# A two-layer attention and token-mixing kernel: the written-out order of its operations is replaced by another

## The chip, the cores and the metric

The kernel runs on one core of a Trainium2 chip. The metric is device time in microseconds of one execution, from the median of several runs. A core has five engines that work at the same time, each through its own list of instructions in order: TensorE (PE in the profile; its weight loads are PEld), VectorE (DVE), ScalarE (ACT), GpSimd (POOL) and SyncE (SP), which here only issues transfers. Engines wait for one another by semaphores.

## The reference

One sequence of 2048 positions and 512 features passes twice through the same two blocks. All tensors are bfloat16.

```python
x = x + A(layernorm(x), wqkv, wo)          # 32 heads of 16, window of 256
x = x + B(layernorm(x), w1, b1, w2, b2)    # mixes along the sequence
...
# A: causal attention in a sliding window
mask = (i - j >= 0) & (i - j < 256)
p = softmax(where(mask, q @ k.T * Dh**-0.5, -1e9))
o = p @ v ; return o @ wo
# B: MLP over positions, 1792 hidden
h = layernorm(x)
u = gelu(einsum("bsd,sf->bdf", h, w1) + b1)
y = (einsum("bdf,fs->bds", u, w2) + b2).transpose(0, 2, 1)
```

## The kernel before

All of x stays on the chip as 16 tiles of 128 positions. Each layer runs as follows.

*Normalising.* For each tile VectorE takes the statistics (L478, L480), GpSimd raises the variance to the power -1/2 (L491), VectorE scales (L498). Transposed tiles, xhT, come from DMA transposes (L549), and for the first two tiles from TensorE (L556) with a copy on ScalarE (L569) or VectorE (L567).

*Projections.* TensorE multiplies (L520, the helper through which nearly all full-size matmuls go). Results leave PSUM by a cast of queries (VectorE L585, ScalarE L587), of keys (L610, L612) and of values (L651, L653). Keys are spread into a block-diagonal form, kbd, either straight from PSUM (VectorE L600, ScalarE L595) or from a staging tile by GpSimd or VectorE (L626) or by eight small transfers (L620). Values pass through transfers too (L656).

*Attention.* The queries are cut into chunks of 256 or 512 positions. For each chunk and each group of heads TensorE makes scores into two pairs of PSUM banks (L710, four matmuls side by side in the rows of the array, each with two heads' keys of 64 positions), ScalarE takes the exponential of each pair (L725), GpSimd or VectorE masks the blocks at the window's edges (L746), TensorE multiplies by the values (L767), and VectorE transposes and divides (L787, L791, L793, L798; L793 can be GpSimd's). The output projection is L520 again, added to x by VectorE (L809).

*Mixing.* The product with w1 is cut along the sequence. Parts of it are computed while attention still runs and are kept in float32 in space that is free then (L520, taken out by L873, L875 or L877), so that TensorE has something to do when it would wait for ScalarE; the last part is L888, added by VectorE (L899) and passed through gelu by ScalarE (L903). The product with w2 is L520 again and is added to x by VectorE (L929, and L915 for the last tile, which is cut into three). In the second layer the tiles of the first layer's w2 product feed the next attention chunk by chunk. Weights w1 and w2 are loaded by SP (L823, L835) into a few buffers; results leave by L976 and L918.

*The order.* A recorder, `Graph`, collects 2475 operations with what they read, write and which buffer pool they take from. Many have `alts`, the same work on another engine. It makes no schedule: `begin_order` unpacks a list that is stored in the text of the kernel, and `replay` walks it. Each entry says which operation comes next and which of its alternatives is taken:

```python
for lo, hi in zip(raw[:n], raw[n:]):
    k, alt = divmod(lo + 256 * hi, 4)
    out.append((left.pop(k), alt))
...
o.eng, o.fn = o.alts[alt][:2]
self._take(o)
```

The walk decides three things: the order in which each engine's instructions stand, the engine of each operation with alternatives, and, since `_take` hands out a pool's free buffers as they come, which buffer each tile gets and so what it must wait for. `emit` then writes each engine's list with the semaphore waits that follow. SP's list is in this order too.

Of the kernel before, what the change touches and what calls it, by code (L numbers as in the profile page):

```python
# [11 lines left out]
P = 128  # L12
# [3 lines left out]
    'c-pmAO^D;>8GhyYy!%bif~F{-fC>sIpnw*%paliApn?`eaX={wXu$^^RPezI4!Gce11h-S4Jx?cg99!o;D8S<%)tj2TyVevALihL3qH7D${c)fVGa}UVGe!e'  # L16
    '@yvK;XR`}QUR$>O>HB-1_j#VrH7;(%00h2#X_%&=>n}cksz0Tk2Vk1EX&Hv`iD8(utAhsG<N7upJFc@>=H|qqw)+_=`-P%!jz**0r@4`-nWh4wsI@wYAPQtK'
    '90-EYmyXXR8q7(V3tu!yv(@By{kYvTIvwBjip8j49@$)h<K#fD<eZOkN48@agxD?-MQ|J<%bdW$`q2f;VXzn+I|b<XJN@GeNebxM*%_s+)oN8JG-95=0MFw$'
    'E=)`U<I(I;o==DK6FQttDV@z`<JF1=fjpj!JOAkP!Iua*O9VQh<S)xbEdmivP6T0GBn6Cqzc0&4ASWb;+a*nNVzMlWX)Dggh{mgGy=GN}rXWaAt5F)&W`s;8'
    '6GFWLaa@<nXM!-Wd=C*7z5jMQIoIuh(Q!T3Xby*F(s!Kaz8~AZZ(0a^QFk20ex7r4x|4HsJ?HAr*e5K@Yr3YW0E#Tj<Rk<NT~$pwodnu=4}vI(_{npC<;3_s'  # L20
    'VSV4HETxXKU|9<@QdO0zhgm5rD{>8YD2TNh$FpoYpjw6IIc%fMtm>uGf1<^55k)1h4Xbq}jv+1&=ZnSn!{M;eXn6CJ$;6%v&GA^*`-72g^$@0h7>;}4aM<nk'
    'x)$zXFc=hz`mr8%Ue)Wm-e@!%UpFFMujO*NW(|K<Dkfs7eW6yW_+mB3`6FA6s_V6?us&Y~e!eM{T#Q1o5J321yFa^!*d$nOoP}lSlc&NTmP<nb`6I%OF|FT<'
    's-ZsC06Eg(njFgm{HBHxRilX5HpMz%_<jJg=X<`HqNOVNPZTFd2&X8>c~jm{q|~|05*?o|#BOKMLEKxN6P07%mnEr5NmQ@Lag?pI;6+fOEcih{yp8XiuWKvc'
    '_dHcm@$x)M;0S=@Ii3Ooy`C;yfUYM=a(0G9R(P4msVDs(ewYvcby)#?#`bz`fDY*-xPfnKe`}DK)GdVGB43#1pQ_cDm6v1B^Fq(JEDwxNZQEuswd%7<jQ|gl'
    'loEmG`5p(wioqG&V9Ih^ZiJ$PiL%^rrKiNGeQ<I?>;|@7335I-R;URC65%8<97oI9YT)RGs_QnVSeh|YrWM;>@U}cv<Ow$(BN${3Euq<LN--{IMOGA970L<H'
    'siOs0&MH{tie*^>T7#l1{HYwmux+WQl#a*oNH7OsSgm&B*ckQu)#{*DsYqxVqL79tk{VdSS6?Y{smgMXbp2@<hFng=0$;G3&7%Mzd@-FO*|C^;KM(U$A_0e~'
    'GW{eu%xbEps-!@OuIq?|>lTquPjWd_7AnnxC&88vmI)wo9HS_dq9i0pyRSA!r}}(0pU=@6^(-h^SylU^5eiQxSpwp>60m%o<BG-N=xZpo+kcm&&1M4)D9feN'
# [982 lines left out]
```

## Time and profile before

| | |
|---|---|
| median of the runs | 435.45 us |
| profiled execution | 435.28 us, of which 433.5 us is the span of its instructions |
| TensorE busy | 421.4 us, 6177 matmuls |
| VectorE busy | 315.7 us, 611 instructions |
| ScalarE busy | 319.0 us, 366 instructions |
| GpSimd busy | 186.3 us, 282 instructions |
| granted TensorE clock | 1.00 |
| transferred by SP's queue | 45.52 MB |

Busy is the time in which at least one instruction of the engine was under way. Matmuls overlap in their pipeline, so a gap between two of them that is shorter than the tail of the first does not show as idle time. An idle engine costs nothing unless it is the one on which the end depends; which one that is changes along the kernel, so the stages are read one by one.

### The profile page before, as it was taken

What the parts mean: (1) busy time and instruction counts of PE and PEld (TensorE: products, weight loads), DVE (VectorE), ACT (ScalarE), POOL (GpSimd) and SP (SyncE); (2) the same over time, 40 slices, a digit from 0 to 9 for tenths busy, and PEclk for the clock granted to TensorE, in tenths of its full rate; (3) what the DMA queues carried; (4) which work ended last, traced back from release to release, by engine and by line L of the source; (5) the groups of instructions that cost most, each with busy time, mean ns of one, the idle gap of its engine ahead of it and who ended that gap; (6) DMA issues with size and microseconds to landing.
All of it is one profiled execution on the core that took longest, in us unless ns stands there. A gap on an engine that the chain in (4) does not pass through costs nothing.

```text
span 433.5 us, 14319 instructions
## 1 busy us (share of the span) xinstructions
PE 421.4 (97%) x6177; PEld 188.8 (44%) x6177; DVE 315.7 (73%) x611; ACT 319.0 (74%) x366; POOL 186.3 (43%) x282
## 2 busy tenths in 40 slices
PE   8889989999999999999999999999999999999997
PEld 7444333434444444444444444444434444444544
DVE  7999888878995988544878898699779667522223
ACT  6999999999997853606999999899999970601000
POOL 4987877455554310010444656776565331000000
PEclk9999999999999999999999999999999999999999
DMA  8983413401064166735472432251222346856514
GB/s 249 175 151 75 87 33 80 101 14 39 15 178 120 52 177 170 215 75 146 107 128 64 95 81 42 50 89 22 45 65 76 88 122 183 218 150 178 149 49 132
DMA packets 104091, 46.44 MB, mean 107 GB/s; under 512 B 34396, under 2 KB 104028, under 8 KB 104028
## 3 DMA queue, kind: packets, MB, share of 16 engines
q1 hardware_dynamic: 104028, 45.52, 42.8%
q8 instruction: 49, 0.80, 0.8%
q14 instruction: 14, 0.11, 0.1%
HBM read 33.56 MB, written 2.10 MB: 82 GB/s over the span
## 4 chain that ended last, share of the span: by engine, by line
PE 83%; ACT 15%; DVE 1%; POOL 1%; issue 0%; POOLq 0%
PE PS L520 57%; ACT pt L725 15%; PE PS L710 9%; PE PS L888 8%; PE PS L767 8%; DVE rl L787 0%; DVE stats L478 0%; DVE xh_sb L498 0%; POOL rstd L491 0%; PE PS L556 0%; PE PS L392 0%; DVE agg L480 0%; POOL ldm L442 0%; DVE ldm L443 0%; DVE x_sb L915 0%
## 5 line engine op out<-in xcount | busy, mean ns | idle before, releaser
L725 ACT ACTIVATE pt<-PS 128x1024 bf16<-128x1024 f32 (+1 forms) x304 | 280.8, 1043 | 10.9 <-PE PS L710 9.8
L746 POOL TENSOR_TENSOR pt<-pt,ldm 128x256 int32<-128x256 int32 (+2 forms) x195 | 128.9, 683 | 90.0 <-ACT pt L725 89.6
L520 PE MATMUL PS<-uT,w2b 128*128 128x512 bf16 (+2 forms) x308 | 69.7, 360 | 0.0
L520 PE MATMUL PS<-xhT,wqkv 128*128 128x512 bf16 (+1 forms) x288 | 67.3, 357 | 2.1 <-ACT pt L725 2.0
L520 PE MATMUL PS<-xh_sb,w1b 128*128 128x512 bf16 x280 | 69.0, 381 | 0.1
L710 PE MATMUL PS<-qT,kbd 32*128 32x64 bf16 (+4 forms) x1552 | 60.2, 247 | 3.5 <-ACT pt L725 1.5
L491 POOL TENSOR_TENSOR rstd<-agg,mhalf 128x2 f32<-128x2 f32 (+1 forms) x33 | 23.1, 703 | 74.8 <-DVE agg L480 74.7
L929 DVE SCALAR_TENSOR_TENSOR x_sb<-PS,bcol,x_sb 128x512 bf16<-128x512 f32 x31 | 22.7, 743 | 39.6 <-PE PS L520 39.6
L787 DVE STREAM_TRANSPOSE rl<-PS 128x1024 f32<-128x1024 f32 x32 | 39.9, 1246 | 14.8 <-PE PS L767 14.7
L710 PEld LDWEIGHTS PS<-qT,kbd 32*128 32x128 bf16 x1552 | 22.5, 92 | 62.4 <-ACT pt L725 47.5
L903 ACT ACTIVATE uT<-rl,bcol 128x512 bf16<-128x512 f32 x28 | 18.4, 713 | 40.7 <-DVE rl L899 40.7
L767 PE MATMUL PS<-pt,vb 64*17 64x128 bf16 (+4 forms) x3104 | 43.8, 248 | 2.3 <-ACT pt L725 0.8
L478 DVE BATCH_NORM_STATS2 stats<-x_sb 128x6 f32<-128x512 bf16 x64 | 42.9, 683 | 0.7
L520 PEld LDWEIGHTS PS<-uT,w2b 128*128 128x128 bf16 x308 | 27.8, 98 | 32.0 <-issue 3.2
L520 PE MATMUL PS<-uT,pt 128*128 128x512 bf16 x168 | 40.9, 379 | 0.0
L767 PEld LDWEIGHTS PS<-pt,vb 64*17 64x17 bf16 x3104 | 31.6, 84 | 17.6 <-issue 7.0
L888 PE MATMUL PS<-xh_sb,w1b 128*128 128x512 bf16 x168 | 38.1, 379 | 0.0
L520 PEld LDWEIGHTS PS<-xh_sb,w1b 128*128 128x128 bf16 x280 | 23.8, 98 | 31.2 <-issue 5.9
L520 PEld LDWEIGHTS PS<-xhT,wqkv 128*128 128x128 bf16 x288 | 23.6, 97 | 29.1 <-issue 6.7
L520 PE MATMUL PS<-wqkv,xhT 128*128 128x512 bf16 x128 | 34.0, 381 | 0.0
L520 PE MATMUL PS<-wo_sb,oT 128*128 128x512 bf16 x128 | 32.7, 381 | 0.6 <-ACT pt L725 0.5
L498 DVE TENSOR_SCALAR xh_sb<-x_sb,agg,rstd 128x512 bf16<-128x512 bf16 x64 | 25.7, 421 | 5.5 <-POOL rstd L491 5.4
(63 smaller groups left out, 336.5 us busy)
## 6 DMA issues: line engine op xcount, KB each, us to landing
w1b<-in_B_w_dram SPq DMA_DIRECT2D x112, 128.0 KB, 2.8
w2b<-in_B_w_dram SPq DMA_DIRECT2D x70, 128.0 KB, 2.7
pt<-in_B_w_dram SPq DMA_DIRECT2D x42, 128.0 KB, 2.9
vb<-vst SPq DMA_DIRECT2D x64, 68.0 KB, 2.1
out_dram<-x_sb SPq DMA_DIRECT2D x15, 128.0 KB, 1.8
x_sb<-in_A_x_dram SPq DMA_DIRECT2D x3, 512.0 KB, 5.8
kbd<-stg SPq DMA_DIRECT2D x88, 16.0 KB, 1.9
wqkv<-in_A_wqkv_dram SPq DMA_DIRECT2D x4, 256.0 KB, 4.8
```

What stands on the lines that cost most here:

```text
L478: op("vector:stat", lambda e: e.bn_stats(st[:, 0:6], x_sb[:, t, :]), reads=[f"x{t}"], writes=[("st", i)], cost=dve_cost(512))
L491: op("gpsimd:rstd", lambda e: e.tensor_tensor(rstd[:, t0:t1, 0], agg[:, t0:t1, 1], mhalf[:, 0:1].to_broadcast([P, t1 - t0]), op=ALU.pow), ...
L498: op("vector:xh", lambda e: e.tensor_scalar(xh_sb[:, t, :], x_sb[:, t, :], agg[:, t, 0:1], rstd[:, t, :], op0=ALU.subtract, op1=ALU.mult), ...
L520: return e.matmul(o, lhsT=w, rhs=x, start=start, stop=stop, skip_group_check=True)
L710: last = e.matmul(bank(tt[r // 2], r % 2)[:, base + c0 * 64:base + (c0 + n) * 64], lhsT=kbd[32 * r:32 * r + 32, tk.slot, o, jj].rearrange( ...
L725: op("scalar:exp", lambda e, ts=ts, tp=tp, i=i, cols=cols: e.activation(probs(tp)[:, i, 0:cols, :], pair(ts)[:, :, 0:cols].rearrange("p r ...
L746: return e.tensor_tensor(v, v, m, op=by)
L767: last = e.matmul(bank(t, h)[32 * r:32 * r + 17, i + q0 * 64:i + (q0 + n) * 64], lhsT=vb[64 * h:64 * h + 64, tk.slot, jj, 4 * o + r, :], r ...
L787: op("vector:od", lambda e, t=tod, tr=tr: e.transpose(rl[:, tr.slot:tr.slot + 2].rearrange("p a b -> p (a b)"), pair(t)), reads=[(tod, i) ...
L888: last = e.matmul(bank(tu, tt), lhsT=v()[:, sc - b0, k0 + tt * P:k0 + (tt + 1) * P], rhs=xh_sb[:, sc, :], start=(sc == b0), stop=(sc == NT ...
L903: op("scalar:gelu", lambda e, ft=ft, tt=tt: e.activation(uT[:, ft, :], rl[:, tmps[tt].slot], ACTF.Gelu_apprx_tanh, bias=b1col[:, ft:ft + 1 ...
L929: op("vector:resy", lambda e: e.scalar_tensor_tensor(x_sb[:, t, :], bank(ft), b2col[:, t:t + 1], x_sb[:, t, :], op0=ALU.add, op1=ALU.add), ...
```

## The change

Nothing but the packed list `ORDER` is replaced: another sequence of the same 2475 operations, with other alternatives chosen for some of them.

```diff
 ORDER = (
-    'c-pmAO^D;>8GhyYy!%bif~F{-fC>sIpnw*%paliApn?`eaX={wXu$^^RPezI4!Gce11h-S4Jx?cg99!o;D8S<%)tj2TyVevALihL3qH7D${c)fVGa}UVGe!e'
...
+    'c-pmAPl)U05g*y#CSQscw4etHXo~`RMFqd2fKn7tK?@2f;D8GXIG}(Idf<Q$4!EEc6<lz^1qT%H!3P(7a6tz@@WBNid~m@B7hLec0Uum&VGr-%!XA8B${srM'
...
 )
```

Unpacked, it comes to this:

| engine | instructions before | after |
|---|---|---|
| TensorE | 6177 | 6177 |
| VectorE | 611 | 630 |
| ScalarE | 366 | 361 |
| GpSimd (without the constants of the preamble) | 278 | 266 |
| SP (transfers) | 438 | 422 |

Of the masks (L746), 60 move from GpSimd to VectorE and 43 from VectorE to GpSimd. Of the products (L793), four go to VectorE and seven to GpSimd. Casts of queries move both ways, four and four; three casts of values and two key expansions move from ScalarE to VectorE; one transposed tile's copy moves from VectorE to ScalarE. Weight loads (L823, L835) and outputs (L976, L918) are issued in another order.

50 lines of the change are left out of this document (25 added, 25 removed).

## The prediction

> **What bounds the kernel now.** I read the page first: busy time and the chain that ended last.
>
> ```profile
> span 433.5 us, 14319 instructions
> ...
> PE 421.4 (97%) x6177; PEld 188.8 (44%) x6177; DVE 315.7 (73%) x611; ACT 319.0 (74%) x366; POOL 186.3 (43%) x282
> ...
> PE 83%; ACT 15%; DVE 1%; POOL 1%; issue 0%; POOLq 0%
> ```
>
> TensorE is occupied for nearly the whole span and carries 83% of the chain; ScalarE has 15%. The profiled execution took 435.28 us, 1.78 more than its span, and the median of the runs shown is 435.45. All sums below start from 435.28. Next I asked for busy time in the stages of the kernel. The columns are length of the stage, then busy time (and instructions) of each engine.
>
> ```profile
> 0.00:9.40 9.40, 8.23 (x82) 7.13 (x83) 6.27 (x25) 5.92 (x9) 4.03 (x15) 1.00 0.78 230
> 9.40:24.00 14.60, 12.57 (x199) 7.06 (x197) 14.03 (x36) 14.60 (x22) 11.99 (x21) 1.00 0.97 218
> 24.00:71.00 47.00, 42.04 (x990) 18.26 (x990) 41.73 (x80) 46.57 (x52) 36.52 (x52) 1.00 0.41 80
> 71.00:126.00 55.00, 54.04 (x1052) 22.38 (x1052) 48.36 (x91) 54.29 (x60) 32.38 (x48) 1.00 0.24 54
> 126.00:157.00 31.00, 31.00 (x587) 13.75 (x581) 25.05 (x49) 27.01 (x29) 11.30 (x15) 1.00 0.41 115
> 157.00:201.00 44.00, 44.00 (x295) 20.18 (x285) 26.63 (x49) 13.26 (x20) 2.26 (x4) 1.00 0.60 162
> 201.00:308.00 107.00, 106.97 (x1791) 44.41 (x1792) 89.01 (x174) 102.40 (x117) 62.19 (x92) 1.00 0.37 75
> 308.00:318.00 10.00, 9.37 (x182) 3.98 (x175) 6.56 (x12) 9.83 (x12) 5.25 (x7) 1.00 0.23 44
> 318.00:354.00 36.00, 35.98 (x656) 15.23 (x653) 26.84 (x52) 34.81 (x38) 18.97 (x28) 1.00 0.34 88
> 354.00:389.00 35.00, 35.00 (x171) 15.88 (x163) 18.45 (x33) 8.32 (x13) 1.38 (x2) 1.00 0.64 177
> 389.00:433.50 44.50, 42.17 (x224) 20.49 (x221) 12.77 (x19) 1.95 (x3) 0.00 (x0) 1.00 0.44 131
> ```
>
> Two regimes stand here. From 9.4 to 126 us ScalarE is full: 14.60 of 14.60, 46.57 of 47, 54.29 of 55 us. After 126 us TensorE is full, except for 0.63 us in 308 to 318 (10.00 - 9.37). The granted clock is 1.00 in every row. The chain in order of time (start, length, what) says the same:
>
> ```profile
> 24.76 9.28 ACT pt L725 x10
> ...
> 43.39 27.65 ACT pt L725 x30
> ...
> 99.16 9.28 ACT pt L725 x10
> ...
> 308.31 9.28 ACT pt L725 x10
> ...
> 389.23 41.95 PE PS L520 x222
> ```
>
> Exponentials (L725) set the time early, at 0.93 us each, with one late patch at 308 us; the rest is matmuls, and the last 42 us is nothing else.
>
> From the stages comes the most that better order can give. TensorE's idle time between its start and its tail is 14.60 - 12.57 = 2.03, 47.00 - 42.04 = 4.96, 55.00 - 54.04 = 0.96, then 0.03, 0.63 and 0.02: 8.63 us in all, 2.0% of 435.28. And most of it can't be had, because it lies where ScalarE is full. ScalarE's own idle time there is 0 + 0.43 + 0.71 = 1.14 us.
>
> **What the change does.** Only the packed list ORDER differs, so I listed both programs engine by engine. TensorE has the same 926 steps, the same 6177 matmuls and the same 337 changes between the three shapes of matmul (projections and MLP, scores L710, probabilities times values L767). The 152 score steps stand in the same sequence. Before 157 us 304 of 311 TensorE steps stand within five places of where they stood. So this is no new plan, it is the old one with neighbours exchanged, and the work of the bounding engine is unchanged: 0 us.
>
> What moves: 60 masks (L746) go from GpSimd to VectorE and 43 the other way; 11 products (L793) change engine; some PSUM evacuations change between VectorE and ScalarE (ScalarE issues 361 instructions instead of 366); two groups of eight key transfers (L620) leave SP's queue, 438 to 422 transfers; and the weight loads (L823, L835) are issued in another order.
>
> **Start-up.** The first exponential starts at 9.40. What leads to it:
>
> ```profile
> 5.71 0.59 ACT L569 COPY xhT<-PS 128x512 bf16<-128x512 bf16 x1 [0.60 <-PE PS L556]
> 5.93 0.61 PE L556 MATMUL PS<-ident,xh_sb 128*128 128x128 bf16 x4
> 6.58 0.42 DVE L567 COPY xhT<-PS 128x512 bf16<-128x512 bf16 x1
> 7.10 1.91 PE L520 MATMUL PS<-xhT,wqkv 128*128 128x256 bf16 x16
> 7.74 0.84 ACT L595 ACTIVATE kbd<-PS,par 128x256 bf16<-128x256 f32 x2 [1.44 <-PE PS L520]
> 8.46 0.37 ACT L587 CAST qT<-PS 128x256 bf16<-128x256 f32 x1
> 8.94 0.40 PE L710 MATMUL PS<-qT,kbd 32*128 32x256 bf16 x12
> 9.40 1.02 ACT L725 ACTIVATE pt<-PS 128x1024 bf16<-128x1024 f32 x1 [0.56 <-PE PS L710]
> ...
> 12.44 0.42 ACT L587 CAST qT<-PS 128x256 bf16<-128x256 f32 x1
> 12.69 4.33 ACT L725 ACTIVATE pt<-PS 128x1024 bf16<-128x1024 f32 x5
> ...
> L600 DVE TENSOR_TENSOR kbd<-PS,par 128x512 bf16<-128x512 f32 x3 | 2.0, 669 | 0.0
> ```
>
> After the change the second copy of xhT is made by ScalarE, 0.59 instead of 0.42, so the first projection starts 0.17 later, at 7.27. In exchange VectorE expands the keys (one L600 of 0.67) while ScalarE casts the query. The second projection step ends 0.6 us of pipeline and 0.44 us of issue after 7.27, at 8.31; the cast of 0.37 ends at 8.72, and L710 starts at 8.82 where it started at 8.94: -0.12. One later cast of a query (12.44 to 12.69, 0.25 us from start to start) leaves ScalarE altogether; since ScalarE is full, that is worth -0.25. One step that could give this back: two score steps now follow each other near 16 us where two projections stood between, but TensorE waits for ScalarE there anyway. Together -0.37; the bounds are 0 and -0.6 (nothing, or both parts and one more such cast).
>
> **The patch at 308 us.** The last exponentials of a chunk hold up L767 for the 0.63 us of TensorE idle time above. The new order puts two w1 steps, four matmuls, ahead of that group, which is more than fills the gap. Three evacuations of values and one of keys also leave ScalarE in 157 to 308:
>
> ```profile
> L653 ACT CAST vst<-PS 128x512 bf16<-128x512 f32 x8 | 4.9, 610 | 15.6 <-PE PS L520 15.6
> L595 ACT ACTIVATE kbd<-PS,par 128x512 bf16<-128x512 f32 x2 | 1.3, 685 | 1.6 <-PE PS L520 1.6
> ```
>
> At 610 and 685 ns these are 3 x 0.61 + 2 x 0.69 = 3.2 us of ScalarE, but TensorE is full where they leave, so they buy slack and no time; if that cover were gone they would be worth their 3.2 us. Between 0 and -0.63 I take -0.4.
>
> **Masks and the two queues.** A mask moved is a mask queued behind other work.
>
> ```profile
> L746 POOL TENSOR_TENSOR pt<-pt,ldm x195: 449/727/1523, 12.6 to 351.4; 128x256 int32<-128x256 int32 x139, 128x128 int32<-128x128 int32 x47, 128x384 int32<-128x384 int32 x9
> L746 DVE TENSOR_TENSOR pt<-pt,ldn x71: 228/414/690, 36.0 to 352.8; 128x256 int32<-128x256 int32 x51, 128x128 int32<-128x128 int32 x17, 128x384 int32<-128x384 int32 x3
> ...
>   PEld PS L767: 2.0, 4
>   PE PS L767: 0.6, 1
> ```
>
> (Duration is least/median/most in ns; below, who waited for masks.) VectorE takes 17 more in net: 2 in the first layer, 15 in the second. At 0.414 us that is 7.0 us more for VectorE and 17 x 0.727 = 12.4 us less for GpSimd. The densest place is 24 to 71 us, where nine masks come to VectorE and two leave: 41.73 + 7 x 0.414 = 44.6 of 47 us. It fits, though what is queued behind a mask there (evacuations of q, k and v, without which a bank isn't free) comes up to 0.69 us later. In the second layer 89.01 + 10 x 0.414 + 4 x 0.69 = 95.9 of 107. Waits for masks cost at most 2.0 us in the whole kernel; I bound the change by that, from -2.0 to +2.0. Since ScalarE doesn't wait for masks but for scores, a short lateness is caught by TensorE's idle time. I take +0.2.
>
> A rule of the Trainium skill speaks against these moves. "SBUF — State Buffer", in its section "SBUF: two separate sides", says that VectorE and GpSimd share one pair of ports, and that a VectorE instruction with two SBUF inputs and a GpSimd instruction that reads SBUF exclude one another for a whole instruction. The trace bears it out only in the tail: the longest VectorE mask, 690 ns, is 276 over the median of 414, and the median is not stretched.
>
> **Transfers.** The new order issues w1 and w2 nearer to their use. What the trace has of them (w1; time to landing least/median/most):
>
> ```profile
> L823 SPq DMA_DIRECT2D w1b<-in_B_w_dram x112: 340/469/1832, 15.4 to 375.2; - x112
> ...
>   PEld PS L520: 0.5, 1
> ...
> DMA to landing us min/median/max: 2.0/2.8/4.6
> ```
>
> One wait of 0.5 us in 112 loads; a load can land 4.6 - 2.8 = 1.8 us later than usual. SP works in order, so a load behind a transfer that still waits for its data waits too: the key transfers, the transposes (L549), and at the end the outputs (L976) behind L929. Late loads would stop TensorE in 157 to 201 or after 354, where nothing covers it. Below, nothing is gained (-0.5, the one wait); above, one load at its latest, +1.8. I take +0.2, as one in 112 was late. The two groups of key transfers that leave SP free its queue early; that is cover for the transposes and no time.
>
> **The end.** The last TensorE group is now seven matmuls of 128 columns instead of five. Ahead of the last small output stands another whole tile's output (L976) where a half tile's (L918) stood.
>
> ```profile
> 431.17 0.81 SPq L918 DMA_DIRECT2D out_dram<-x_sb  x2
> ```
>
> SP needs 0.81 / 2 = 0.4 us to issue one. Between 0 (the last result is later than that) and +0.4 (it waits for a whole issue) I take +0.1; a gain is excluded, since the last group is no shorter.
>
> **Sum:** 435.28 - 0.37 - 0.4 + 0.2 + 0.2 + 0.1 = 435.0 (-0.1%). With all lower ends: 435.28 - 0.6 - 0.63 - 2.0 - 0.5 = 431.6. With all upper ends: 435.28 + 2.0 + 1.8 + 0.4 = 439.5.
>
> **Rivals.**
>
> *The waits only change places.* Each one removed comes back for a neighbour: 435.3. For it: the score sequence is identical and ScalarE stays full from 9.4 to 126. It can't be told from the forecast by time alone.
>
> *VectorE and GpSimd exclude each other.* If each of the 17 extra masks is held for the 276 ns that the longest shows, and TensorE sees all of it, it is 17 x 0.276 = 4.7 us, so 435.0 + 4.7 = 439.7. It decides as soon as VectorE in 24 to 71 us passes 47 us: 44.6 + 9 x 0.276 = 47.1, just there. Against it: only few masks were stretched before. This is the rule of "SBUF — State Buffer" in the Trainium skill, taken at its worst.
>
> *Weight loads come late (the other side).* SP's queue, in 157 to 201 and after 354: if loads are issued so close that a landing of 4.6 instead of 2.8 us stops TensorE each time, five such stops are 5 x 1.8 = 9.0 and one more 0.5: 435.0 + 9.5 = 444.5. It decides when the margin between landing and first use falls under 1.8 us. Against it: a single wait before, and transfers at 0.60 and 0.64 of the DMA engines there.
>
> *TensorE's idle time closes.* All 8.63 us, and the start-up's 0.37: 426.3. For it: the search had the whole order to choose from. Against it: ScalarE is full where 7.95 of the 8.63 us lie, and its work there falls by one cast.
>
> **How the numbers follow.** Forecast 0.60, waits change places 0.16, exclusion 0.15, late loads 0.06, idle time closed 0.03. The range that leaves out no more than 2 in 10 joins the first three: 432.0 to 439.7. Two per cent of 435.45, about what a measurement of this kernel can tell from no change, is 8.7 us. Faster than 426.7 is only the last case, 0.03; slower than 444.2 only late loads, 0.06; within that the rest, 0.91.
>
> **What would show it.** In the new profile: TensorE's count stays 6177 and its busy time is within 2 us of 421.4; the first L725 starts near 9.3; ScalarE stays over 98% busy from 24 to 126 us; TensorE's idle time in the patch near 308 us falls under 0.3; VectorE's total rises to about 324 us and GpSimd's falls to about 178; waits of TensorE for masks stay under 4 us, for weight loads under 2. I am wrong if the ScalarE-bound stretch ends more than 2 us away from 126, or if TensorE shows gaps in 157 to 201 or after 354.

## The result, and the profile after

The changed kernel takes 437.10 us (median of six; 436.80 to 437.38). The kernel before, on the same chip, takes 435.45 us as the median of five runs; a sixth run of it took 591.89 us and is left out. The ratio is 1.0037, 95% interval 1.0023 to 1.0051: slower by about 1.6 us, where 0.3 us less was forecast. The profiled execution took 437.18 us, 1.90 more than that of before. First the page after:

```profile
span 435.4 us, 14241 instructions
...
PE 412.6 (95%) x6109; PEld 188.1 (43%) x6177; DVE 326.7 (75%) x630; ACT 317.4 (73%) x361; POOL 182.4 (42%) x270
...
PE 72%; ACT 18%; DVE 3%; DMA 2%; issue 2%; POOL 1%; SPq 1%
```

All 6177 weight loads are there, but the records of 68 matmuls are not, so TensorE's busy time is not compared with the 421.4 of before; starts of weight loads are used instead. What can be read: VectorE, a transfer, GpSimd and "issue" now stand in the chain with 8% together, where they had 2%. The same stages as in the prediction (length, then busy time and instructions of each engine) show where:

```profile
9.40:24.00 14.60, 12.71 (x221) 7.41 (x221) 14.29 (x36) 14.48 (x21) 11.36 (x20) 1.00 1.01 213
24.00:71.00 47.00, 40.17 (x937) 17.69 (x940) 42.21 (x84) 45.63 (x50) 31.59 (x45) 1.00 0.47 84
71.00:126.00 55.00, 52.15 (x1018) 22.10 (x1018) 46.88 (x82) 54.37 (x60) 38.74 (x58) 1.00 0.26 54
...
308.00:318.00 10.00, 9.75 (x218) 4.31 (x201) 7.96 (x14) 9.84 (x12) 3.59 (x6) 1.00 0.24 46
```

ScalarE, the bound there, lost 0.94 us in 24 to 71 (46.57 to 45.63) and nothing in 71 to 126 (54.29, 54.37). Its timeline (start, length, what; in brackets the idle time before) names the moments. Before:

```profile
24.76 18.44 ACT L725 ACTIVATE pt<-PS 128x1024 bf16<-128x1024 f32 x20 [0.24 <-PE PS L710]
43.39 3.77 ACT L725 ACTIVATE pt<-PS 128x1024 bf16<-128x1024 f32 x4 [0.19 <-PE PS L710]
```

After:

```profile
23.31 4.68 ACT L725 ACTIVATE pt<-PS 128x1024 bf16<-128x1024 f32 x5
28.30 5.60 ACT L725 ACTIVATE pt<-PS 128x1024 bf16<-128x1024 f32 x6 [0.31 <-PE PS L710]
34.20 3.77 ACT L725 ACTIVATE pt<-PS 128x1024 bf16<-128x1024 f32 x4 [0.29 <-PE PS L710]
38.46 5.61 ACT L725 ACTIVATE pt<-PS 128x1024 bf16<-128x1024 f32 x6 [0.49 <-PE PS L710]
44.34 2.86 ACT L725 ACTIVATE pt<-PS 128x1024 bf16<-128x1024 f32 x3 [0.28 <-PE PS L710]
```

One run of 20 exponentials has become runs of 6, 4 and 6: three holes, each a wait for scores. Exponentials in a run start 0.905 us apart; by starts the holes are 0.47, 0.45 and 0.63 us. (I call hole what a distance has over 0.905.) Both kernels have a fourth, at 43.4 and 44.3. All holes over 0.1 us from 24 to 126 us sum to 2.4 us before and 3.9 after, without the place near 118 us where a copy stands between two exponentials.

The sequence of score steps is the same in both kernels, so their starts make a ledger. Stretches are cut at score steps that start at 8.9, 19.7, 26.0, ... us in the kernel before; each entry is the longer (+) or shorter (-) time of the stretch against the kernel before, worked out from the starts in the traces. The rows with numbers are the experiments below:

| profile | 0–8.9 | –19.7 | –26.0 | –46.4 | –66.5 | –121.7 | –205.8 | –313.1 | –349.7 | –last weight load | sum |
|---|---|---|---|---|---|---|---|---|---|---|---|
| after | -0.15 | -0.34 | -0.01 | **+1.52** | +0.12 | +0.10 | -0.20 | +0.01 | +0.30 | +0.42 | +1.76 |
| after, 2nd profile (15) | -0.39 | -0.35 | -0.01 | **+1.45** | +0.12 | +0.17 | -0.22 | +0.44 | +0.29 | +0.39 | +1.90 |
| 1 start new, rest old | +0.10 | -0.35 | -0.01 | +2.41 | 0.00 | -0.06 | +0.36 | 0.00 | +0.04 | +0.01 | +2.49 |
| 2 middle old | +0.58 | -0.30 | -0.01 | +1.73 | +0.12 | +0.08 | -0.20 | -0.01 | +0.30 | +0.18 | +2.47 |
| 3 copy first | +0.83 | -0.34 | -0.01 | **+0.83** | +0.13 | +0.16 | -0.22 | -0.03 | +0.29 | +0.30 | +1.94 |
| 4 w2 piece early | +0.08 | -0.16 | -0.01 | +1.36 | +0.12 | +0.10 | -0.23 | +0.15 | +0.29 | +0.21 | +1.89 |
| 5 large load later | -0.39 | -0.35 | -0.01 | **+0.78** | +0.12 | +0.22 | -0.15 | +0.52 | +0.29 | +0.04 | +1.09 |
| 6 before, copy late | +0.04 | 0.00 | 0.00 | **+0.86** | +0.01 | +1.65 | +0.13 | -0.04 | +0.03 | +0.01 | +2.70 |
| 7 before, large load late | 0.00 | 0.00 | +0.02 | +0.04 | +0.01 | +0.05 | -0.04 | -0.02 | +0.03 | 0.00 | +0.08 |
| 8 four repairs | -0.30 | -0.14 | +0.14 | +0.61 | +0.12 | +0.08 | +0.27 | +0.41 | +0.29 | 0.00 | +1.48 |
| 9 six repairs | +0.21 | -0.34 | -0.01 | +0.84 | +0.12 | +0.14 | +0.33 | +0.02 | +0.29 | +0.32 | +1.93 |
| 10 seven repairs | +0.57 | -0.35 | -0.01 | +1.67 | +0.10 | +0.07 | -0.22 | -0.02 | +0.30 | +0.11 | +2.23 |
| 11 less on VectorE | -0.23 | +0.13 | -0.01 | +1.32 | +0.10 | +0.14 | -0.09 | 0.00 | +0.30 | +0.25 | +1.90 |
| 12 no hurry last | -0.32 | +0.75 | -0.01 | **+0.01** | **+2.51** | +0.10 | -0.15 | +0.04 | +0.29 | +0.23 | +3.44 |
| 13 loads as before | -0.36 | +0.05 | -0.01 | +1.50 | +0.12 | +0.16 | -0.22 | +0.01 | +0.29 | +0.46 | +1.99 |
| 14 before, new loads | +0.50 | +0.46 | -0.03 | +0.05 | 0.00 | 0.00 | +1.11 | -0.01 | +0.03 | +0.01 | +2.12 |
| 16 run 9, then before | +0.82 | -0.35 | -0.01 | +0.84 | +0.12 | +7.79 | -0.08 | -0.02 | +0.01 | 0.00 | +9.11 |

Rows are single executions. Where the order up to a place is the same, 26 to 46 us gives +1.36 to +1.52 (after, 15, 4, 13), and the stretches that end at 66.5, 121.7 and 349.7 agree within 0.2 us. The others do not repeat: the first two lie between -0.39 and +0.83 and between -0.35 and +0.75 in thirteen profiles of one and the same start, and 122 to 313 us and the tail differ by up to 0.6 us. Of the 1.76 us of the changed kernel 1.52 are made in 26 to 46 us; 0.30 lie in 313 to 350, 0.42 in the tail.

What is late at each hole? Hole 1, TensorE:

```profile
26.41 0.46 PE L767 MATMUL PS<-pt,vb 64*17 64x64 bf16 x27
27.28 0.64 PE L767 MATMUL PS<-pt,vb 64*17 64x256 bf16 x37 [0.41 <-issue]
```

It stops after 27 of the 64 products that stand there in a row, ahead of its 345th weight load of the program, and waits for nothing that the profile shows. Weight loads there are 0.76 us apart, and the score step stands right behind. Hole 2: a score step behind a product of L767 that waited for a GpSimd mask. Hole 3: a score step behind projections that waited for a copy of queries on VectorE. The table of waits from 24 to 46 us has the last two (total, times, longest), and the two timelines show why the copy, L585, was late: two normalizations stand ahead of it.

```profile
PE PS L520 <- DVE qT L585: 0.8, 1, 0.8
...
PE PS L767 <- POOL pt L746: 0.6, 1, 0.6
```

```profile
33.83 1.25 DVE L787 STREAM_TRANSPOSE rl<-PS 128x1024 f32<-128x1024 f32 x1 [0.64 <-PE PS L767]
35.01 1.37 DVE L498 TENSOR_SCALAR xh_sb<-x_sb,agg,rstd 128x512 bf16<-128x512 bf16 x2
36.30 0.68 DVE L585 CAST qT<-PS 128x512 bf16<-128x512 f32 x1
```

```profile
37.04 1.04 PE L520 MATMUL PS<-xhT,wqkv 128*128 128x512 bf16 x4 [0.83 <-DVE qT L585]
38.01 0.40 PE L710 MATMUL PS<-qT,kbd 32*128 32x192 bf16 x12
```

The two normalizations are also longer than usual. VectorE in the kernel before, then GpSimd in the changed one:

```profile
34.49 0.74 DVE L498 TENSOR_SCALAR xh_sb<-x_sb,agg,rstd 128x512 bf16<-128x512 bf16 x2
```

```profile
35.05 1.19 POOL L746 TENSOR_TENSOR pt<-pt,ldm 128x128 int32<-128x128 int32 x2
```

The same pair takes 0.74 us there and 1.37 here, where two GpSimd masks run beside it. One by one they last 0.64 and 0.81 us, and each ends 0.15 us after one of the masks ends (masks 35.50 and 36.23, normalizations 35.65 and 36.38). So 0.63 us of the copy's lateness is VectorE held up beside GpSimd. That is read from the durations; no run below moves these two masks away.

Counted by how late the score steps are, the 1.52 us are about 0.4 around hole 1, 0.35 around hole 2 and 0.8 around hole 3.

### The profile page after: what moved, and what is told of

The parts are those of the page before. It is cut to its first block, busy times and chain, and to the rows that moved or that the text cites. A ratio compares the mean times of both kernels' runs of the same rounds, so it can differ in the third digit from the quotient of the medians.

```text
span 435.4 us, 14241 instructions
## 1 busy us (share of the span) xinstructions
PE 412.6 (95%) x6109; PEld 188.1 (43%) x6177; DVE 326.7 (75%) x630; ACT 317.4 (73%) x361; POOL 182.4 (42%) x270
## 4 chain that ended last, share of the span: by engine, by line
PE 72%; ACT 18%; DVE 3%; DMA 2%; issue 2%; POOL 1%; SPq 1%
PE PS L520 49%; ACT pt L725 18%; PE PS L888 8%; PE PS L710 8%; PE PS L767 7%; DMA x_sb<-in_A_x_dram 1%; DVE stats L478 1%; DMA pt<-in_B_w_dram 1%; POOL pt L746 1%; DVE rl L787 1%; DVE xh_sb L498 1%; POOL rstd L491 0%; SPq L407 0%; DVE vst L651 0%; POOL kbd L626 0%
## 5 line engine op out<-in xcount | busy, mean ns | idle before, releaser
L746 POOL TENSOR_TENSOR pt<-pt,ldm 128x256 int32<-128x256 int32 (+2 forms) x178 | 120.5, 694 | 103.0 <-ACT pt L725 102.3
L520 PE MATMUL PS<-xhT,wqkv 128*128 128x512 bf16 (+1 forms) x268 | 64.4, 355 | 5.4 <-issue 1.9
L520 PE MATMUL PS<-xh_sb,w1b 128*128 128x512 bf16 x264 | 66.1, 380 | 2.4 <-issue 1.7
L520 PE MATMUL PS<-uT,w2b 128*128 128x512 bf16 (+2 forms) x297 | 67.1, 359 | 1.0 <-issue 0.6
L787 DVE STREAM_TRANSPOSE rl<-PS 128x1024 f32<-128x1024 f32 x32 | 39.9, 1246 | 14.8 <-PE PS L767 14.5
L491 POOL TENSOR_TENSOR rstd<-agg,mhalf 128x2 f32<-128x2 f32 (+1 forms) x33 | 23.5, 717 | 61.0 <-DVE agg L480 60.9
L767 PE MATMUL PS<-pt,vb 64*17 64x128 bf16 (+4 forms) x3104 | 44.3, 248 | 1.5 <-issue 0.6
L746 DVE TENSOR_TENSOR pt<-pt,ldn 128x256 int32<-128x256 int32 (+2 forms) x88 | 37.9, 441 | 6.1 <-ACT pt L725 5.8
L767 PEld LDWEIGHTS PS<-pt,vb 64*17 64x17 bf16 x3104 | 32.0, 84 | 17.3 <-issue 7.4
L888 PE MATMUL PS<-xh_sb,w1b 128*128 128x512 bf16 x165 | 38.1, 379 | 0.2
L520 PE MATMUL PS<-wo_sb,oT 128*128 128x512 bf16 x120 | 31.4, 380 | 2.5 <-ACT pt L725 1.4
L520 PE MATMUL PS<-wqkv,xhT 128*128 128x512 bf16 x121 | 32.7, 380 | 0.9 <-issue 0.6
```

The costliest lines, as they stand in the source:

```text
L491: op("gpsimd:rstd", lambda e: e.tensor_tensor(rstd[:, t0:t1, 0], agg[:, t0:t1, 1], mhalf[:, 0:1].to_broadcast([P, t1 - t0]), op=ALU.pow), ...
L520: return e.matmul(o, lhsT=w, rhs=x, start=start, stop=stop, skip_group_check=True)
L746: return e.tensor_tensor(v, v, m, op=by)
L767: last = e.matmul(bank(t, h)[32 * r:32 * r + 17, i + q0 * 64:i + (q0 + n) * 64], lhsT=vb[64 * h:64 * h + 64, tk.slot, jj, 4 * o + r, :], r ...
L787: op("vector:od", lambda e, t=tod, tr=tr: e.transpose(rl[:, tr.slot:tr.slot + 2].rearrange("p a b -> p (a b)"), pair(t)), reads=[(tod, i) ...
L888: last = e.matmul(bank(tu, tt), lhsT=v()[:, sc - b0, k0 + tt * P:k0 + (tt + 1) * P], rhs=xh_sb[:, sc, :], start=(sc == b0), stop=(sc == NT ...
```

## The experiments

All edits are made in the unpacked list; its entries are named by engine and line. Ratios are to the kernel before, run beside them; the ledger above has each profile. Many of the intervals overlap one another, so the causes are read from the ledger and the timelines, and the ratios only say whether the whole got faster or slower.

**1 and 2: halves of the two orders.**

```diff
 1: entries 1-193 as changed, the rest as before
 2: as changed; of entries 194-300 the computing ones in before's order, on before's engines
```

> The changed order up to the score step before 26.4 us (193 operations of the list), then the order and engines of the kernel before. Theory 'three holes' (the loss of the change sits in three idle stretches of ScalarE at 27.3, 33.9 and 37.9 us, 0.46, 0.46 and 0.62 us by start-to-start times, and the start-up gain of about 0.5 us is kept by whatever follows): no such hole appears, the score steps from 30 to 120 us run 0.4 to 0.7 us ahead of the kernel before, and the time is 435.1 (ratio 0.999). Rival 'swallowed' (a gain at the start goes into the next wait of TensorE): the score steps are back at the kernel before's times by 126 us, time 435.6. Rival 'the loss is in transfers that the new start-up leaves late': the score steps are behind the kernel before by 40 us, time 436.5 or more.

> The changed kernel, with the computing operations of one stretch (list places 193 to 300, about 26.4 to 44 us) put in the order and on the engines of the kernel before; the transfers and everything else stay as changed. Theory 'three holes': ScalarE runs through without the three holes, the score steps after 46 us are 1.2 to 1.6 us earlier than in the changed kernel, time 435.6 (ratio to the kernel before 1.000). Rival 'amount of work on the mask engines / two engines in each other's way over the whole stretch to 126 us': the steps are earlier by 0.3 at most, time 436.8 to 437.2.

Measured: 1.0045 (1.0030 to 1.0060) and 1.0038 (1.0024 to 1.0052). Both missed, and the joint itself is the main reason (in run 2 the stop of hole 1 stays as well, 0.84 us, since the transfers were left as changed). VectorE of run 1:

```profile
27.37 0.68 DVE L478 BATCH_NORM_STATS2 stats<-x_sb 128x6 f32<-128x512 bf16 x1
27.97 0.91 DVE L498 TENSOR_SCALAR xh_sb<-x_sb,agg,rstd 128x512 bf16<-128x512 bf16 x1
28.80 0.18 DVE L480 BATCH_NORM_AGGREGATE agg<-stats 128x2 f32<-128x9 f32 x1
28.90 0.64 DVE L478 BATCH_NORM_STATS2 stats<-x_sb 128x6 f32<-128x512 bf16 x1
29.47 1.22 DVE L787 STREAM_TRANSPOSE rl<-PS 128x1024 f32<-128x1024 f32 x1
```

The start of the changed order leaves normalizations undone that the old order did earlier; joined, they stand ahead of L787, which frees the bank of the next score step. L787 had its input near 27.5 and starts at 29.47; ScalarE gets a hole of 1.63 us. In run 2 L787 starts at 30.00 behind the same work, and TensorE waits 1.30 us for it. So these runs don't test the three holes, but show the same thing larger: 2.1 us of unhurried work ahead of an urgent instruction, in it a normalization of 0.91 us beside GpSimd's masks.

**3: the copy ahead of the two normalizations** (hole 3 alone).

```diff
 VectorE, near 35 us
-L498 L498 L585
+L585 L498 L498
```

> The changed kernel with one thing moved: VectorE copies out the query block of line 585 ahead of the two normalizations of line 498 that stand before it near 35 us. Theory 'the copy is late because of its place in VectorE's queue': TensorE's wait of 0.83 us at 36.2 us goes, ScalarE's third hole (0.62 at 37.9 us) goes, score steps from 40 to 120 us come 0.5 to 0.7 earlier than in the changed kernel, time 436.5. Rival 'the scores were late for another reason' (a mask, a transfer or an instruction fetch near 34 us): the hole stays, time 437.1.

Measured: 1.0018 (1.0005 to 1.0031). ScalarE's hole 3 is gone:

```profile
29.25 15.03 ACT L725 ACTIVATE pt<-PS 128x1024 bf16<-128x1024 f32 x16 [0.28 <-PE PS L710]
44.64 2.85 ACT L725 ACTIVATE pt<-PS 128x1024 bf16<-128x1024 f32 x3 [0.35 <-PE PS L710]
```

Its stretch is +0.83 instead of +1.52, and of the 0.69 us between, about 0.5 are won at hole 3 and 0.2 at hole 2, counted by the score steps. By starts, 0.28 of hole 2 and 0.11 of hole 3 are left, which the merged line doesn't show. The time, 437.08, misses the 436.5 that was expected. In its profile the first stretch, which scatters, is 0.98 us longer than in that of the changed kernel, and the order is the same there.

**4: the late piece of w2**, five places earlier in SP's list.

> The changed kernel with one transfer moved: the w2 piece that landed at 413.58 us, 0.6 us after TensorE came to its product, is issued five places earlier in SyncE's queue, near 407.3 instead of 409.9. Theory: the wait of 0.6 us goes, all that follows ends 0.4 to 0.6 earlier, time 436.6. Rival 'another piece of w2 becomes the late one, since the transfer engines are shared': the wait moves to the next pieces, time 437.0 to 437.3.

Measured: 1.0031 (1.0020 to 1.0042); the tail is +0.21 instead of +0.42. Inconclusive: the same tail order gave +0.04 and +0.46 in runs 5 and 13.

**5: the large load behind the transposes** (hole 1 alone).

```diff
 SP, near 20 us
-L422 L549 L549 L549
+L549 L549 L549 L422
```

> The changed kernel with one transfer moved: the 512 KB load of the output projection's weights (line 422, first used near 48 us) is issued behind the three transposes that follow it, near 22.5 us instead of 19.7. In the changed kernel TensorE stops for 0.76 us inside one product, at its 345th weight load (27.28 us); the 16 KB instruction packet that starts at 23.93 us, when the 512 KB load lands (24.01), is the one that it needs. Theory 'late instructions': the packet now starts by 22.5, the stop inside the product is gone, ScalarE's first hole (0.47 us at 28.3) is gone, later score steps come 0.4 to 0.5 earlier counted from the first score step, time 0.4 below the changed kernel. Rival 'the stop is a matter of the products or of their data': the stop stays at the 345th weight load, no change.

Measured: 1.0016 (1.0007 to 1.0025). The stop is gone, and so is hole 1; the stretch is +0.78 instead of +1.52:

```profile
26.17 0.84 PE L767 MATMUL PS<-pt,vb 64*17 64x64 bf16 x64
27.03 0.40 PE L710 MATMUL PS<-qT,kbd 32*128 32x192 bf16 x12
```

```profile
23.06 10.19 ACT L725 ACTIVATE pt<-PS 128x1024 bf16<-128x1024 f32 x11
33.48 3.77 ACT L725 ACTIVATE pt<-PS 128x1024 bf16<-128x1024 f32 x4 [0.23 <-PE PS L710]
```

Of the 0.74 us between, counted by the score steps, about 0.4 are won at hole 1 and the rest at holes 2 and 3, whose steps come less late.

What TensorE waited for are its own instructions. The table of DMA queues counts them (packets, MB, share). I take q8 for TensorE's, since its 12,559 instructions (weight loads, matmuls, waits) over 49 packets are 256 each, and 0.80 MB / 49 = 16 KB. In the changed kernel, over the whole span, then from 21 to 23.9 us, then from 23.9 to 25.9 us:

```profile
q8 instruction: 49, 0.80, 0.8%
```

```profile
q1 hardware_dynamic: 1104, 0.64, 84.5%
q14 instruction: 1, 0.01, 1.3%
```

```profile
q1 hardware_dynamic: 452, 0.11, 209.0%
q8 instruction: 1, 0.02, 6.0%
```

Between 21 and 23.9 us no packet of q8 starts, just after 23.9 one does. The single records (us):

| | large load issued | TensorE 256 instructions ahead of the stop's place | packet starts | ends | TensorE comes to the place | goes on |
|---|---|---|---|---|---|---|
| before | 19.01 | 22.04 | 23.35 | 24.83 | 26.86 | 26.86 |
| after | 19.69 | 21.09 | 23.93 | 25.87 | 26.52 | **27.28** |
| after, 2nd profile | 19.76 | 20.89 | 23.81 | 25.57 | 26.27 | **27.00** |
| run 3 | 21.06 | 22.08 | 25.26 | 26.93 | 27.50 | **28.23** |
| run 1 | 21.84 | 21.33 | 22.32 | 23.53 | 26.76 | 26.76 |
| run 5 | 24.71 | 20.89 | 21.84 | 22.93 | 26.27 | 26.28 |
| run 7 | 21.07 | 22.04 | 24.83 | 25.83 | 26.87 | **27.30** |

When the 512 KB load has been issued 1.0 to 1.4 us before TensorE passes the earlier place, the packet starts 2.7 to 3.2 us after that passage; this holds for seven of all eighteen profiles, and they are the seven with the stop. In the others, where the load was issued about 3 us before or came later, it is 0.9 to 1.8. TensorE goes on 1.3 to 1.5 us after the packet's end, wherever it stops. The Trainium skill, "Runtime: NRT & Kernel Launch", section "Instruction fetch mechanics", says that instructions stream in blocks of 16 KiB (256 instructions), the next fetched while the current one runs, and that this is mostly hidden. Size and count agree with the trace; only one of the 49 stopped TensorE inside a step.

**6 and 7: the two causes put into the kernel before.**

```diff
 6: VectorE, near 35 us
-L585 ... L791 ... L746 ... L498
+L791 L746 L498 L585
 7: SP, near 19 us
-L422 L549 L823
+L549 L823 L422
```

> The kernel before with the suspected cause put in: on VectorE, a reciprocal of line 791, a mask of line 746 and a normalization of line 498 (together some 1.1 us) are put ahead of the copy of line 585 that runs at 35.16 us. Theory 'place in VectorE's queue': TensorE's next query block waits, the score step that starts at 36.83 us comes 0.5 to 0.9 late, ScalarE gets a hole of 0.4 to 0.7 us near 38 us, time 0.4 to 0.7 above the kernel before (ratio 1.0010 to 1.0016). Rival 'a short lateness is caught by the idle time of TensorE', the step of the prediction: no hole, ratio 1.000.

> The kernel before with the other suspected cause put in: its 512 KB load of line 422 is issued two places later in SyncE's queue, so that it lands near 25 us instead of 23.51. TensorE asks for the next 16 KB of instructions at 22.0 us; the packet started at 23.35 us in the kernel before. Theory 'late instructions': the packet starts near 24.8 to 25.3, TensorE stops for 0.7 to 1.3 us at its 345th weight load near 26.9 us, ScalarE gets a hole of as much, time 0.4 to 1.0 above the kernel before (ratio 1.001 to 1.002). Rival: the packet doesn't wait for the load, no stop, ratio 1.000.

Run 6: 1.0022 (1.0010 to 1.0033). VectorE, TensorE, ScalarE:

```profile
35.72 1.13 DVE L498 TENSOR_SCALAR xh_sb<-x_sb,agg,rstd 128x512 bf16<-128x512 bf16 x1
36.77 1.27 DVE L585 CAST qT<-PS 128x512 bf16<-128x512 f32 x2
```

```profile
37.51 0.60 PE L520 MATMUL PS<-xhT,wqkv 128*128 128x512 bf16 x2 [1.04 <-DVE qT L585]
38.05 0.40 PE L710 MATMUL PS<-qT,kbd 32*128 32x192 bf16 x12
```

```profile
38.50 5.61 ACT L725 ACTIVATE pt<-PS 128x1024 bf16<-128x1024 f32 x6 [0.76 <-PE PS L710]
```

The hole is made at will, 1.03 us by starts, +0.86 in the stretch; both are larger than was expected. The three instructions put ahead would take 1.1 us by their usual lengths but took 1.6: the normalization lasts 1.13 us where it took 0.40 in the kernel before. GpSimd's L793 runs beside it from 35.59 to 36.70 us, and the normalization ends 0.15 us after that. (The +1.65 in 66 to 122 is a key transfer that TensorE waited 1.7 us for; this execution was the longest of the twelve, so it is not the rule.) Run 7: 1.0000 (0.9989 to 1.0011). The stop appears at the 345th weight load, 0.43 us, so the cause of the stop is right, but the time does not move, against the expectation: the score step behind it is 0.18 us late against its neighbours, and no exponential waits. Lateness is caught, then, up to a point. The step of hole 1 loses 0.68 us and leaves a hole of 0.47, that of run 6 loses 1.17 and leaves 1.03: 0.1 to 0.2 us are caught, and the rest is a hole of ScalarE.

**8 to 12: repairs on top of each other.** Each run moves what the one before showed as the next wait. All five missed the time that their theory gave.

```diff
 8: 3, 4 and 5 together; GpSimd, near 31 us
-L491 L746 L746
+L746 L746 L491
 9: SP: L422 and one L823 behind the four L656;
    VectorE: one L798 behind L610
 10: VectorE, near 39 us
-L798 L498 L498 L651
+L651 L798 L498 L498
 11: two VectorE masks L746 (36.6, 41.9 us) on GpSimd; one L798 behind L651, L585
 12: VectorE: two L498 and that L798 to 50-60 us; L626 behind L787; four masks L746 near 54 us on GpSimd
```

> The changed kernel with four repairs: the 512 KB load behind the transposes (first hole), GpSimd's root of line 491 behind the two masks that stand after it near 31 us (second hole), the copy of line 585 ahead of the two normalizations of line 498 (third hole), and the late piece of w2 five places earlier. Theory 'late instructions and queue places': the three holes of ScalarE are gone (its holes between 24 and 126 us sum to 2.3 to 2.5 us as in the kernel before, against 3.92), time 1.6 to 2.0 below the changed kernel, ratio to the kernel before 0.998 to 1.000. Rival 'each repair only uncovers the next wait': the holes sum to 3.3 or more, ratio 1.002 or more.

Measured: 1.0017 (1.0003 to 1.0030). Hole 1 is gone, hole 3 is 0.30 at 39.5, hole 2 still 0.32: its product now waits for the transfers of L656, landed at 31.76 where the mask had come at 32.02. The stretch is +0.61, so together the three repairs win 0.91 us, less than runs 3 and 5 added up.

> The changed kernel with the repairs of the second four-repair run and two more: the 512 KB load of line 422 and the w1 piece after it are issued behind the four transfers of line 656 (in the four-repair run these landed at 31.76 us and the product of line 767 waited for them where it had waited for the mask), and the sum of line 798 stands behind the key copy of line 610 (a score step at 39.05 us had waited for that copy). Theory 'late instructions and queue places, each with a next one behind it': both waits go, ScalarE's holes between 24 and 126 us sum to 2.3 to 2.6 us, the stretch from 26 to 46 us takes no more than 0.2 us longer than in the kernel before (four-repair run +0.61, changed kernel +1.52), ratio to the kernel before 0.9995 to 1.0010. Rival 'there is always a next wait in this order': the stretch stays 0.5 or more longer, ratio 1.0015 or more.

Measured: 1.0014 (1.0004 to 1.0023). The three holes are gone, one of 0.80 is there at 41.7: a copy, L651, behind L798 and two L498. The stretch is +0.84, no better than in run 8.

> The changed kernel with the six repairs and a seventh: the copy of line 651 that ran at 39.96 us stands ahead of the sum of line 798 and the two normalizations of line 498 that delayed it (in the six-repair run TensorE's next block waited for that copy, and ScalarE had a new hole of 0.80 us at 41.7). Theory 'queue places, each with a next one behind it, and a finite number of them': the hole at 41.7 goes, ScalarE's holes between 24 and 126 us sum to 2.5 us or less, the stretch from 26 to 46 us takes at most 0.2 us longer than in the kernel before, ratio 1.000 to 1.0008. Rival 'this order has always a next wait': the stretch stays 0.5 us or more longer, ratio 1.0012 or more.

Measured: 1.0040 (1.0027 to 1.0053). ScalarE runs through for 22 exponentials, then pays: TensorE waits 1.2 us for a VectorE mask (L746) that stands behind two L798 and two L498.

```profile
23.10 20.27 ACT L725 ACTIVATE pt<-PS 128x1024 bf16<-128x1024 f32 x22
44.73 1.94 ACT L725 ACTIVATE pt<-PS 128x1024 bf16<-128x1024 f32 x2 [1.37 <-PE PS L710]
```

> The seven-repair kernel with work taken off VectorE: its two masks of line 746 that ran at 36.6 and 41.9 us (together 1.36 us) go to GpSimd, which is busy 4.6 of the 8 us from 38 to 46, and the sum of line 798 that stood ahead of the two copies near 42.7 us stands behind them. Theory 'VectorE's work is what is left': with every place in the queue repaired, the seven-repair kernel had only shifted its hole to 44.7 us (1.71) because VectorE is busy 7.89 of the 8 us from 38 to 46; with 1.4 us less to do there, the hole goes, ScalarE's holes between 24 and 126 us sum to 2.6 us or less, the stretch from 26 to 46 us takes 0.0 to 0.3 us longer than in the kernel before, ratio 1.000 to 1.001. Rival 'this order has always a next wait, whatever VectorE has to do': a hole of 0.5 us or more stays, ratio 1.0015 or more.

Measured: 1.0034 (1.0024 to 1.0044). The hole, 1.13 us, moves to 46.1: L787 stands behind L798, L498 and two L626, and these two take 1.28 us beside GpSimd's masks where they took 0.60 in run 10.

> The kernel of the run with less work on VectorE, with what is in no hurry put behind what is: two normalizations of line 498 that ran at 42.9 and 45.6 us (their results are read after 65 and 79 us) and a sum of line 798 (read at 65 us) stand behind the copies that score steps wait for, the parity product of line 626 behind the bank's release of line 787, and four masks of line 746 near 54 us are on GpSimd again as in the kernel before. Theory 'work without hurry ahead of urgent work on VectorE is the whole loss of the stretch': no hole from 26 to 47 us beyond the 0.5 us near 43.4 that the kernel before has too, holes between 24 and 126 us 2.6 us or less, stretch from 26 to 46 us within 0.2 us of the kernel before, ratio 1.000 to 1.001. Rival 'the order has always a next wait': a hole of 0.5 us or more more than the kernel before, ratio 1.0015 or more.

Measured: 1.0070 (1.0052 to 1.0088). 26 to 46 us takes as long as in the kernel before (+0.01), so the moves of runs 8 to 12 (queue places, transfers, two masks to GpSimd) make good the whole loss of that stretch. But they do it by putting work off, and what was put behind is due in the next, where a normalization that waits for GpSimd's L491 holds up a copy again:

```profile
57.63 0.80 DVE L498 TENSOR_SCALAR xh_sb<-x_sb,agg,rstd 128x512 bf16<-128x512 bf16 x1 [0.58 <-POOL rstd L491]
58.35 0.68 DVE L585 CAST qT<-PS 128x512 bf16<-128x512 f32 x1
```

```profile
59.09 0.60 PE L520 MATMUL PS<-xhT,wqkv 128*128 128x512 bf16 x2 [1.34 <-DVE qT L585]
```

Busy time from 26 to 46 and from 46 to 66 us (TensorE, its loads, VectorE, ScalarE, GpSimd), in the kernel before and in run 12:

```profile
26.00:46.00 20.00, 18.13 (x484) 8.50 (x484) 18.66 (x36) 19.81 (x22) 14.94 (x20) 1.00 0.39 87
46.00:66.00 20.00, 17.79 (x348) 6.99 (x346) 16.42 (x29) 20.00 (x23) 16.70 (x26) 1.00 0.29 58
```

```profile
26.00:46.00 20.00, 17.92 (x484) 8.42 (x487) 17.77 (x34) 19.84 (x23) 17.62 (x25) 1.00 0.58 108
46.00:66.00 20.00, 15.73 (x326) 6.17 (x326) 18.08 (x33) 17.81 (x20) 11.57 (x17) 1.00 0.33 73
```

VectorE does 0.89 us less in the first and 1.66 more in the second, and ScalarE's 2.19 us of idle time are there. VectorE is the second bound of this part: 18.66 of 20 us busy in the kernel before, beside a ScalarE with 19.81.

**13 and 14: the order of the first loads, alone.**

```diff
 13: as changed, first loads as before; 14: as before, first loads as changed
-x, x, x, w, w, w, x     (x: L407, w: L411; order of before)
+x, x, w, x, w, x, w     (changed order)
```

> The changed kernel with the first loads in the order of the kernel before (two exchanges: lines 407 and 411). First score step so far: 8.94 to 8.98 us in three profiles of the old order of loads, 8.55 to 9.77 in seven of the new one; one product at 10 us waits 0.4 to 1.0 us for a weight piece that the exchange put later. Theory 'the new order of loads only scatters the start': first score step at 8.8 to 9.0, no wait of TensorE for a load near 10 us, time 0.0 to 0.3 below the changed kernel and a narrower spread of runs. Rival 'the new order of loads is the gain of the start': the score step at 19.7 us comes 0.3 or more later than in the changed kernel (19.25), time 0.3 above it.

> The kernel before with the changed order of the first loads alone (two exchanges, lines 407 and 411). The reverse exchange in the changed kernel cost it 0.40 us between the first score step and 19.7 us. Theory 'the order of loads is the gain of the start by itself': the score step at 19.74 us comes 0.3 to 0.4 earlier, ratio 0.999. Rival 'the gain needs the changed order of the products too': the product of line 520 that ran at 9.27 us waits 0.8 us for its weight piece, which lands near 10.1, the score step at 19.74 comes no earlier, ratio 1.000 to 1.001.

Measured: 13 is 1.0036 (1.0023 to 1.0049), 14 is 1.0016 (1.0004 to 1.0028). In run 13 the stretch to 19.7 us is +0.05 where the changed kernel has -0.34, and in run 14 it is +0.46: TensorE waits 1.1 us for weights. Whether the order of the loads carries the gain of the start is not shown by this. With the new loads TensorE waits near 10 us for a piece of the weights, and the stretch follows that wait: -0.34 with a wait of 0.4 us, about -0.15 with 0.6, +0.13 with 0.9 (run 11) and +0.75 with 1.5 (run 12), though all have the same order up to there. One profile each says nothing against that scatter. Another 1.11 us of run 14 lie in 122 to 206 us, where TensorE waits 0.9 us for a load of w1.

**15: the changed kernel once more.**

> The changed kernel itself, unmodified, beside the others on the same chip. Theory 'late instructions': the stop inside the product at the 345th weight load recurs, with the 16 KB packet starting within 0.2 us of the landing of the 512 KB load, and the three holes of ScalarE recur with 0.4 to 0.7 us each; ratio 1.003 to 1.004. Rival 'one disturbed execution': stop and holes are elsewhere or gone, ratio nearer to 1.001.

Measured: 1.0030 (1.0019 to 1.0040). Stop and holes recur: 0.73 us between the weight loads, holes of 0.44, 0.45 and 0.60.

**16: run 9 up to 76 us, then the order of before.**

> The repaired order of the run beside it up to about 76 us, the order and engines of the kernel before from there. Theory: it keeps the 0.34 us that the changed order gains between the first score step and 20 us, pays nothing in 26 to 46 us, and none of the 0.3 us that the changed order loses between 325 and 350 us, nor the 0.4 at the end: 0.1 to 0.4 below the kernel before, ratio 0.999 to 1.000. Rival 'gains of the start are lost in the stretch from 122 to 206 us' (a run with the changed start lost 0.35 there): ratio 1.000 to 1.001.

Measured: 1.0197 (1.0182 to 1.0211). TensorE waits 6.2 us once for a transpose (L549). Near 76 us SP comes to a w1 load and waits 8.4 us for its buffer, and the transpose stands behind it. The total tests neither theory; but from 122 us to the end the stretches are within 0.1 us of the kernel before, so the 0.3 us in 313 to 350 belong to the changed order of that part.

## Why the prediction was wrong

The time lies inside the range, 432.0 to 439.7, but the forecast was 0.1% faster and it is 0.37% slower. The 8.7 us that the prediction takes for what a measurement can tell are far too wide: the interval here is 0.6 us to either side. By its own steps:

- **Start-up, -0.37.** The changed kernel's profile has -0.15 to the first score step and -0.34 from there to 19.7 us, and the first exponential starts at 9.24 where 9.28 was worked out. That is luck: in thirteen profiles of this same start the two entries together lie between -0.74 and +0.49, for the first score step starts anywhere from 8.55 to 9.77 us (8.93 to 8.98 in three profiles of the old start) and TensorE waits 0.4 to 1.5 us for weights near 10 us. I had credited a cast that leaves ScalarE and had not looked at the order of the first loads.
- **Patch at 308 us, -0.4.** TensorE's idle time fell from 0.63 to 0.25 as foretold, but no time was won: 205.8 to 313.1 changed by 0.01 (by +0.44 in the second profile), 313.1 to 349.7 by +0.30 in both. The 0.3 us come with the changed order of that part, by run 16; I did not take them apart.
- **Masks and the two queues, +0.2. This step failed.** "Since ScalarE doesn't wait for masks but for scores, a short lateness is caught by TensorE's idle time." It is caught up to 0.1 or 0.2 us (runs 6 and 7). TensorE's idle time cannot serve, because TensorE works in order: while it waits for a mask or a copied bank, the score step behind it waits as well, and ScalarE, the bound, idles. I had added up VectorE's work (44.6 of 47 us; it came to 42.21) where its order decided. Holes 2 and 3 come from this and hold about 1.15 of the stretch's 1.52 us by the score steps; run 3 wins 0.69 by moving one copy, and run 6 makes the like of hole 3 in the kernel before. Part of it is the other mechanism that the prediction weighed: 0.63 us of hole 3's lateness is two normalizations drawn out beside GpSimd's masks.
- **Transfers, +0.2.** I looked for late weights. None stopped TensorE for long in the changed kernel's profile (0.4 us near 10 us, 0.25 at 413.6). What a transfer did make late were TensorE's instructions: hole 1, about 0.4 us of the 1.52 by the score steps, and 0.74 by run 5, whose repair eased holes 2 and 3 too. The sum had no term for that.
- **The end, +0.1.** From the start of the last weight load to the end of the span it takes 2.78 us after and 2.65 before, +0.13: right. The 0.42 ahead of it scatter from 0.00 to 0.46 with nearly the same order.
- **What would show it.** VectorE 326.7 us (foretold 324) and GpSimd 182.4 (foretold 178, where the 12.4 us less of the prediction's own count would give 173.9) were near; the first exponential and the patch were right; waits for masks came to 1.6 us at L767, the step that the prediction read, but to 4.3 in all of TensorE's rows, over the 4 of the sign. ScalarE was to stay over 98% busy from 24 to 126 us: it was 45.63 + 54.37 of 102, 98.04%, against 98.9% before. So the sign passed, though the 0.86 us that it lost are nearly half of the slowdown; it was set too wide to tell.
- **Rivals.** The times of exclusion of VectorE and GpSimd, 439.7, late weight loads, 444.5, and closed idle time, 426.3, did not come. The mechanism of the first did, in part, and not where it was looked for: not in masks but in normalizations ahead of a copy. "Waits only change places" was nearest in mechanism, but not at 435.3: in a part with two nearly full engines the places are not equal.

Hole 2 was closed only together with others (runs 9 to 12), so its own price is not measured. No version with the changed order beats the kernel before; the nearest, run 9, is at 1.0014 (1.0004 to 1.0023).

## What to carry to other kernels

Where one engine bounds a stretch and is fed by an in-order engine, ask of every wait of the feeder what stands behind it, and how much lateness the bound's buffers catch; here it was 0.1 to 0.2 us. On a helper engine that is over 90% busy, look at which work is in a hurry, not at the sum: three instructions without hurry, put ahead of a copy that TensorE needs, took 1.6 us and cost 0.86 us. And look at how long such work takes beside its neighbours in time, not only at its usual length: one of the three took 1.13 us instead of 0.40. And check a moved large transfer for what it delays beyond its own data, instructions included.

## What the runs showed of the hardware

TensorE's instructions come in packets of 16 KB on a queue of their own, and they can be late. Where a 512 KB load had been issued 1.0 to 1.4 us before TensorE passed the place 256 instructions earlier, the packet started 2.7 to 3.2 us after that passage instead of 0.9 to 1.8. TensorE ran dry for 0.43 to 0.84 us at the same instruction in all seven profiles with that timing. The stop appears as "issue", with no releaser.

VectorE and GpSimd can hold each other up, and here it reached the path. A normalization, L498, took 0.41 us in most cases. In the changed kernel four of the 64 took 0.53 to 0.81 us, each beside a GpSimd mask, and each ended 0.15 us after a mask ended; so did the one of 1.13 us in run 6, beside GpSimd's L793. Two of the four stand ahead of the copy of hole 3. Masks are drawn out as well: worked out from the records of the changed kernel, a VectorE mask of 128 x 256 took 498 ns (median of 15) when GpSimd was busy for more than 70% of it and 414 (of 36) when for less than 20%; of 128 x 128, 762 (of 4) against 278 (of 14). Together that is 15 x 0.084 + 4 x 0.484 = 3.2 us of VectorE in the whole kernel; none of the changed kernel's three holes waited for a mask that VectorE made. Copies out of PSUM are not drawn out: L585 took 676 ns (median of 14) with GpSimd busy and 682 (of 5) without.

The rule of the Trainium skill that the prediction weighed ("SBUF — State Buffer", section "SBUF: two separate sides") says that a VectorE instruction with two SBUF inputs and a GpSimd instruction that reads SBUF exclude one another for a whole instruction. It is visible after all in the masks, as the 498 and 762 ns above show.
